# Filling the edges of the second batch's value tile from GpSimd, ahead of the loads into the tile

## Chip, cores, metric

One core of one Trainium2 chip. The metric is the device time of one execution in microseconds, the median of several.

## The reference

Attention with a window of 32 and eight global tokens over 8 batches, 8 heads, 576 tokens of 64, then a gated feed-forward layer over all 4608 tokens:

```python
scores = scale * q @ k.T ; masked outside |i-j| <= 32 unless row or column is global
attn = softmax(scores) @ v                    # 8 x 8 x 576 x 64
x = attn.transpose(0, 2, 1, 3).reshape(4608, 512)
ffn_out = (gelu(x @ w_gate) * (x @ w_val)) @ w_out      # 512 -> 1536 -> 512
out = x + sigmoid(x @ w_res) * ffn_out
```

## The kernel before

The kernel runs in nine chunks of 512 tokens. For chunk c, TensorE does the feed-forward input products (`ffn_in`, twelve column blocks), then its output products (`ffn_out`), between which the attention of chunk c+1 is woven. The kernel puts TensorE's results into tiles in PSUM, and uses such a tile again once another engine has read it. Batch b's values lie in tile `ve[b % 2]`, with a column of ones per head (for the softmax sum) and zeroed edges; `vo` is a copy of it shifted by 64 tokens. The parts that matter (cuts are marked `# ...`):

```python
def load_v(b):                       # five loads, f32 in HBM -> bf16, on GpSimd's queue
    t = ve[b % 2]
    for c in range(5):
        # ... rows p0:p1 of block c
        nc.gpsimd.dma_start(t[p0:p1, c, :, 0:D], v[b].rearrange("h s d -> s h d")[s0 + p0:s0 + p1])

def shift_v(b):                      # copy within the chip's memory, SyncE's queue
    nc.sync.dma_start(vo[b % 2][0:64, 0:4, :, :], ve[b % 2][64:128, 0:4, :, :])
    nc.sync.dma_start(vo[b % 2][64:128, 0:4, :, :], ve[b % 2][0:64, 1:5, :, :])

def zero_rest(i, eng):
    eng.memset(ve[i][:, :, :, D:VG], 1.0)
    eng.memset(ve[i][0:32, 0, :, :], 0.0)
    eng.memset(ve[i][96:128, 4, :, :], 0.0)
    eng.memset(gt[i][:, 0:64], 0.0)
    eng.memset(gt[i][:, 64 + S:128 + S], 0.0)
    eng.memset(ptg[i][:, :, 64 * (i % 2):64 * (i % 2) + 64], 0.0)
# ...
load_qk(1)                           # all on GpSimd's queue, in this order
load_gate_cols(1024, 1536)           # last third of wg_t and wv_t
load_v(1)
nc.gpsimd.dma_start(wr_t, moe_w_res.rearrange("(kt p) n -> p kt n", p=128))
for h0 in range(0, NFF, 6):          # wo_t in two halves
    nc.gpsimd.dma_start(wo_t[:, h0:h0 + 6, :], moe_w_out.rearrange("(kt p) n -> p kt n", p=128)[:, h0:h0 + 6, :])
for n in range(1, B // 2):
    for what in "kqv":
        gather(what, n)              # nine gathers
# ... attention of chunk 0
for c in range(NCH):
    # ... transposes of q and k of batch c+1 (SyncE); load_v(c+1) if c > 0
    for j in range(NFF):
        ffn_in(c, j)                 # g_ps, v_ps on TensorE; gelu on ScalarE; ht = gsb * v_ps on VectorE
        if c == 0 and j == 1:        # (shortened)
            zero_rest(1, nc.vector)
            hot_rows(1)
        # ... at j == 8: shift_v(c+1), load_qk(c+2), copies qz of q
    # 16 slots: scores, global rows (sn), values (nd) and transposes (xt) of chunk c+1,
    # each followed by one of: r_ps (gate), f_ps in three groups of four matmuls; four times
```

At the end of `ffn_out` VectorE makes `prb`, GpSimd adds `ob = prb + xtok`, and SyncE's queue stores `ob`. The transposes `xt` of the next chunk stand on that same queue between the stores.

The softmax here doesn't subtract the row's maximum and nothing guards it: scores larger than these inputs give would overflow.

Of the kernel before, what the change touches and what calls it, by code (L numbers as in the profile page):

```python
# [23 lines left out]
def kernel(  # L24
# [12 lines left out]
    nc = tc.nc  # L37
# [48 lines left out]
    def load_qk(b):  # L86
        for src, dst in ((q, q_st), (k, k_st)):
            for r in range(NQT):
                n = min(128, S - 128 * r)
                nc.gpsimd.dma_start(dst[0:n, r, :].rearrange("p (h d) -> p h d", d=D),  # L90
                                    src[b].rearrange("h s d -> s h d")[128 * r:128 * r + n])

    def load_v(b):
        t = ve[b % 2]
        for c in range(5):
            p0, p1 = (32, 128) if c == 0 else (0, 96) if c == 4 else (0, 128)
            s0 = 128 * c - 32
            nc.gpsimd.dma_start(t[p0:p1, c, :, 0:D],  # L98
                                v[b].rearrange("h s d -> s h d")[s0 + p0:s0 + p1])

    def shift_v(b):
        nc.sync.dma_start(vo[b % 2][0:64, 0:4, :, :], ve[b % 2][64:128, 0:4, :, :])
        nc.sync.dma_start(vo[b % 2][64:128, 0:4, :, :], ve[b % 2][0:64, 1:5, :, :])

    def load_gate_cols(n0, n1):
        for src, dst in ((moe_w_gate, wg_t), (moe_w_val, wv_t)):
            nc.gpsimd.dma_start(dst[:, :, n0:n1], src.rearrange("(kt p) n -> p kt n", p=128)[:, :, n0:n1])
# [46 lines left out]
    def zero_qk(i):  # L154
        for u in range(2):
            zero_wide(qz[i], 64 - 64 * u, 64, u * S, [[2 * S, NP], [1, S]])
        zero_wide(kt[i], 0, 128, 0, [[S + 64, NP], [1, 32]])
        zero_wide(kt[i], 0, 128, 32 + S, [[S + 64, NP], [1, 32]])
# [9 lines that stand above are left out]
    def zero_globals(b0, b1):  # L168
        zero_wide(kgz, 0, 128, b0 * NP * 128, [[1, (b1 - b0) * NP * 128]])
        zero_wide(qgz, 0, 128, b0 * NP * 16, [[1, (b1 - b0) * NP * 16]])  # L170
# [58 lines left out]
    def hot_rows(i):  # L229
        r0 = 64 - 64 * (i % 2)  # L230
        nc.scalar.copy(gt[i][r0:r0 + 64, 64:64 + S], hot[r0:r0 + 64, :])
# [6 lines left out]
    def double_qk(n0, n1):  # L238
        for what in "kq":
            nc.vector.tensor_copy(twice[what][:, n0:n1, :, :],  # L240
                                  view(gath[what], 0, 128, n0 * D, [[D, n1 - n0], [0, 2], [1, D]]))

    def spread_qk(n0, n1):
        nn = n1 - n0
        for what, big, pstep in (("k", kgz, 144), ("q", qgz, 16)):
            tg = pss.tile([128, nn, 128], BF16, name="tg", tag="sc")
            for n in range(nn):
                nc.tensor.transpose(tg[:, n, :], twice[what][:, n0 + n, :, :].rearrange("p a d -> p (a d)"), ident)
            width = big.shape[2] * big.shape[3]
            for e in range(2):  # L250
                shift = 64 * e if what == "k" else 0
                for u in range(2):
                    (nc.scalar.copy if what == "q" else nc.vector.tensor_copy)(
                        view(big, 64 * u, 64, (2 * n0 + e) * width + shift + 8 * u,
                             [[2 * width, nn], [pstep, NP], [1, NG]]),
                        view(tg, 64 * u, 64, 64 * e + 8 * u, [[128, nn], [16, NP], [1, NG]]))

    def spread_v(n0, n1):
        nc.vector.tensor_copy(vgb[:, n0:n1, 0:D], gath["v"][:, n0:n1, :])

    def spread_vg(b, eng):
        r0 = 64 * (b % 2)
        eng.tensor_tensor(vgs[r0:r0 + 64, b, :].rearrange("p (h e) -> p h e", e=VG),
                          view(vgb, r0, 64, (b // 2) * VG, [[0, H], [1, VG]]),
                          view(diag, r0, 64, 0, [[1, H], [0, VG]]), ALU.mult)
# [32 lines left out]
    def turn_qk(b):  # L298
        for src, dst, c0 in ((q_st, qt[b % 2], 0), (k_st, kt[b % 2], 32)):
            for r in range(NQT):  # L300
                n = min(128, S - 128 * r)
                nc.sync.dma_start(dst[:, :, c0 + 128 * r:c0 + 128 * r + n], src[0:n, r, :], transpose=True)

    def prep_qz(b, p0, p1):
        for u in range(2):
            nc.vector.tensor_copy(qz[b % 2][64 * u:64 * u + 64, p0:p1, u, :],  # L306
                                  qt[b % 2][64 * u:64 * u + 64, p0:p1, :])
# [93 lines left out]
    def ffn_in(c, j):  # L401
        x = xt[c % 2]
        g_ps = psm.tile([128, 512], F32, name="g_ps", tag="mm")
        for kk in range(NKT):
            nc.tensor.matmul(g_ps, wg_t[:, kk, 128 * j:128 * j + 128], x[:, kk, :],  # L405
                             start=(kk == 0), stop=(kk == NKT - 1))
        v_ps = psm.tile([128, 512], F32, name="v_ps", tag="mm")
        for kk in range(NKT):
            nc.tensor.matmul(v_ps, wv_t[:, kk, 128 * j:128 * j + 128], x[:, kk, :],  # L409
                             start=(kk == 0), stop=(kk == NKT - 1))  # L410
        gsb = work.tile([128, 512], BF16, name="gsb", tag="gsb", bufs=3)
        nc.scalar.activation(gsb, g_ps, ACTF.Gelu, bias=0.0, scale=1.0)  # L412
        nc.vector.scalar_tensor_tensor(ht[:, j, :], gsb, 0.5, v_ps, ALU.mult, ALU.mult)  # L413
# [58 lines left out]
    global_rows(0)  # L472
    load_qk(1)
    load_gate_cols(1024, 1536)
    load_v(1)
    nc.gpsimd.dma_start(wr_t, moe_w_res.rearrange("(kt p) n -> p kt n", p=128))
    for h0 in range(0, NFF, 6):
# [17 lines left out]
    for c in range(NCH):  # L495
        b = c + 1
        if b < B:
            if c == 0:
                zero_qk(1)
            turn_qk(b)  # L500
            if b > 1:
                load_v(b)
        held = None
        for j in range(NFF):
            ffn_in(c, j)
            if b < B:
                if c == 0:
                    if j == 1:
                        zero_rest(1, nc.vector)
                        hot_rows(1)  # L510
                    elif j == 2:
                        zero_globals(2, B)
                        spread_vg(1, nc.vector)
                if c == 1:
                    if j == 3:
                        double_qk(1, B // 2)
                    elif j == 6:
                        spread_qk(1, B // 2)
                        spread_v(1, B // 2)
                    elif j == 8:  # L520
                        for n in range(2, B):
                            spread_vg(n, nc.gpsimd)
                if j == 8:
                    shift_v(b)
                    if b + 1 < B:
                        load_qk(b + 1)
                    prep_qz(b, 0, NP)
                if j == 11:
                    held = global_scores(b)
        slots = {n: [] for n in range(16)}  # L530
        if c + 1 < NCH:
            if held is not None:
                slots[0].append(lambda: global_exp(b, *held))
                slots[4].append(lambda: global_rows(b))
            for n in range(8):
                slots[n].append(lambda n=n: scores(c + 1, n // 4, n % 4))
            for t in range(4):
                slots[5 + 2 * t].append(lambda t=t: values(c + 1, t))
                slots[7 + 2 * t].insert(0, lambda t=t: turn_x(c + 1, t))
        work_f = [w for t in range(4) for w in ffn_out(c, t)]  # L540
        for n in range(16):
            for w in slots[n]:
                w()
            work_f[n]()
# [30 lines left out]
```

## Time and profile before

| | before |
|---|---|
| time, median (range) | 433.5 us (432.9 to 435.0, 4 runs) |
| span in the profile | 431.6 us |
| TensorE busy | 386.6 us, 90% |
| VectorE, ScalarE, GpSimd busy | 49%, 39%, 39% |
| TensorE idle for ht, from 44 us on | 20.2 us |
| granted clock at one half | 20.5 us, from 47.6 to 68.1 |

In the profile, a wait reads "who <- for whom: us in total, times, longest"; a timeline row reads "start, duration, engine, line of the kernel, operation, written <- read, count", with the idle time ahead of it in brackets. PE is TensorE, DVE VectorE, ACT ScalarE, POOL GpSimd, SPq SyncE's DMA queue; `in_v` is v in HBM, the chip's main memory. The granted clock is the share of its full clock that TensorE was given. The lines for the stall are in the prediction. One more view is needed for the comparison, SyncE's queue in the kernel before:

```profile
62.00 0.47 SPq L102 DMA_DIRECT2D vo<-ve  x1
...
85.65 0.38 SPq L440 DMA_DIRECT2D out_dram<-ob  x1
88.03 1.21 SPq L393 DMA_TRANSPOSE xt<-xtok  x1
```

The first store goes out 2.4 us before the first transpose: here the store does not hold the transpose up.

### The profile page before, as it was taken

The page shows a single profiled execution, that of the slowest core. Times are in us where ns is not written, and L with a number is a line of the kernel's source. Part 1 is how long each engine was busy: PE and PEld are TensorE (multiplying, and loading weights), DVE is VectorE, ACT ScalarE, POOL GpSimd, SP SyncE. Part 2 cuts the span into 40 slices and gives each one's busy share as a digit, 9 for nine tenths or more (in the row PEclk, how much of TensorE's full clock was granted, in tenths as well). Part 3 has the DMA queues.
Part 4 walks back from the last instruction along what each step waited for, and adds up shares of the span by engine and source line. Part 5 has one row for each costly group of instructions (what it writes and reads, how often), then busy time and mean ns, then how long its engine had stood idle before and what let it go on. Part 6 is the DMA issues. An engine that isn't in the chain of part 4 may idle for free.

```text
span 431.6 us, 7189 instructions
## 1 busy us (share of the span) xinstructions
PE 386.6 (90%) x2749; PEld 208.9 (48%) x2794; DVE 209.6 (49%) x396; ACT 169.6 (39%) x274; POOL 167.9 (39%) x194
## 2 busy tenths in 40 slices
PE   2578009999999999999999999999999999999995
PEld 1363004654465446544654565456545654564442
DVE  6774027554656355535544554356435644463421
ACT  5455002623462336333623462345235423533320
POOL 6577252915492471257125712561330120022012
PEclk9999758999999999999999999999999999999999
DMA  7999998949997999399849992996296130021001
GB/s 173 169 178 155 161 164 170 109 93 112 146 92 111 101 178 120 66 124 182 88 87 112 185 89 77 128 184 73 74 147 93 38 98 1 0 75 62 0 26 74
DMA packets 164642, 46.56 MB, mean 108 GB/s; under 512 B 152128, under 2 KB 158784, under 8 KB 164608
## 3 DMA queue, kind: packets, MB, share of 16 engines
q0 software_dynamic: 108784, 18.62, 60.5%
q1 hardware_dynamic: 55824, 27.48, 33.0%
q8 instruction: 22, 0.36, 0.4%
q14 instruction: 12, 0.10, 0.1%
HBM read 39.19 MB, written 9.44 MB: 113 GB/s over the span
## 4 chain that ended last, share of the span: by engine, by line
PE 74%; issue 8%; POOL 1%; DVE 1%; POOLq 0%; DVEq 0%
PE f_ps L432 19%; PE v_ps L409 18%; PE g_ps L405 17%; PE r_ps L422 6%; PE nd L373 4%; PE sc L347 3%; PE nd L367 2%; PE sn L335 2%; PE sg L313 2%; POOL ob L438 1%; PE ss L318 1%; DVE qz L306 1%; PE tx L397 0%; POOLq L570 0%; DVE ht L413 0%
## 5 line engine op out<-in xcount | busy, mean ns | idle before, releaser
L409 PE MATMUL v_ps<-xt,wv_t 128*128 128x512 bf16 x431 | 111.8, 382 | 21.0 <-DVE ht L413 20.4
L412 ACT ACTIVATE gsb<-g_ps 128x512 bf16<-128x512 f32 x108 | 64.5, 597 | 145.8 <-PE g_ps L405 112.4
L413 DVE SCALAR_TENSOR_TENSOR ht<-gsb,v_ps 128x512 bf16<-128x512 bf16 x108 | 73.9, 687 | 91.7 <-PE v_ps L409 90.1
L438 POOL TENSOR_TENSOR ob<-prb,xtok 128x512 f32<-128x512 f32 x36 | 41.9, 1164 | 193.3 <-DVE prb L436 193.2
L405 PE MATMUL g_ps<-xt,wg_t 128*128 128x512 bf16 x415 | 109.4, 381 | 1.1 <-ACT xt L398 0.7
L432 PE MATMUL f_ps<-wo_t,ht 128*128 128x512 bf16 x412 | 102.0, 380 | 1.0
L409 PEld LDWEIGHTS <-wv_t 128*128 128x128 bf16 x432 | 42.5, 98 | 72.5 <-issue 22.3
L405 PEld LDWEIGHTS <-wg_t 128*128 128x128 bf16 x432 | 42.4, 98 | 52.0 <-issue 1.9
L432 PEld LDWEIGHTS <-ht 128*128 128x128 bf16 x432 | 38.4, 98 | 34.0
L350 ACT ACTIVATE pt<-sc 128x512 bf16<-128x512 f32 x72 | 41.8, 597 | 29.1 <-PE sc L347 29.0
L425 ACT ACTIVATE rsb<-r_ps 128x512 bf16<-128x512 f32 x36 | 21.4, 596 | 62.0 <-PE r_ps L422 58.0
L352 DVE TENSOR_TENSOR pt<-pt,maskw 128x512 bf16<-128x512 bf16 x72 | 31.8, 444 | 26.7 <-ACT pt L350 25.6
L90 POOL DMA_DIRECT2D q_st<-in_q_dram x35 | 29.8, 868 | 24.0 <-DMA qt<-q_st 24.0
L436 DVE SCALAR_TENSOR_TENSOR prb<-rsb,f_ps 128x512 f32<-128x512 bf16 x36 | 24.6, 684 | 29.4 <-PE f_ps L432 29.2
L422 PE MATMUL r_ps<-wr_t,xt 128*128 128x512 bf16 x137 | 36.6, 379 | 0.4
L98 POOL DMA_DIRECT2D ve<-in_v_dram x40 | 34.3, 869 | 1.9 <-DMA k_st<-in_k_dram 1.9
L90 POOL DMA_DIRECT2D k_st<-in_k_dram x35 | 30.8, 908 | 2.8 <-issue 1.2
L347 PE MATMUL sc<-qz,kt 128*128 128x128 bf16 x288 | 27.8, 224 | 0.0
L347 PEld LDWEIGHTS <-kt 128*128 128x128 bf16 x288 | 21.7, 100 | 12.1
L387 DVE TENSOR_TENSOR xtok<-nd,rden 128x512 bf16<-128x512 f32 x34 | 23.5, 692 | 1.2
L373 PEld LDWEIGHTS <-pt 128*128 128x128 bf16 x576 | 22.3, 97 | 1.8 <-DMA vo<-ve 0.8
L373 PE MATMUL nd<-ve,pt 128*128 128x65 bf16 x320 | 22.4, 193 | 0.0
(104 smaller groups left out, 259.7 us busy)
## 6 DMA issues: line engine op xcount, KB each, us to landing
out_dram<-ob SPq DMA_DIRECT2D x36, 256.0 KB, 2.1
vo<-ve SPq DMA_DIRECT2D x16, 260.0 KB, 5.7
q_st<-in_q_dram POOLq DMA_DIRECT2D x28, 128.0 KB, 5.0
k_st<-in_k_dram POOLq DMA_DIRECT2D x28, 128.0 KB, 6.1
ve<-in_v_dram POOLq DMA_DIRECT2D x24, 128.0 KB, 6.7
ve<-in_v_dram POOLq DMA_DIRECT2D x16, 96.0 KB, 6.0
wg_t<-in_moe_w_gate_dram POOLq DMA_DIRECT2D x3, 512.0 KB, 5.9
wv_t<-in_moe_w_val_dram POOLq DMA_DIRECT2D x3, 512.0 KB, 12.7
```

The source lines that it names most:

```text
L90: nc.gpsimd.dma_start(dst[0:n, r, :].rearrange("p (h d) -> p h d", d=D), src[b].rearrange("h s d -> s h d")[128 * r:128 * r + n])
L98: nc.gpsimd.dma_start(t[p0:p1, c, :, 0:D], v[b].rearrange("h s d -> s h d")[s0 + p0:s0 + p1])
L347: nc.tensor.matmul(sc[:, n, :, :], kt[b % 2][:, p, 64 * i:64 * i + 128], qz[b % 2][:, p, :, 64 * i:64 * i + 64], start=True, stop=True)
L350: nc.scalar.activation(mine, sc, ACTF.Exp, bias=0.0, scale=SCALE)
L373: nc.tensor.matmul(nds[h // 4][:, VG * (h % 4):VG * (h % 4) + VG], view(pt, 0, 128, c0, [[1, 128]]), vw, start=False, stop=(h % 4 == 3 and ...
L405: nc.tensor.matmul(g_ps, wg_t[:, kk, 128 * j:128 * j + 128], x[:, kk, :], start=(kk == 0), stop=(kk == NKT - 1))
L409: nc.tensor.matmul(v_ps, wv_t[:, kk, 128 * j:128 * j + 128], x[:, kk, :], start=(kk == 0), stop=(kk == NKT - 1))
L412: nc.scalar.activation(gsb, g_ps, ACTF.Gelu, bias=0.0, scale=1.0)
L413: nc.vector.scalar_tensor_tensor(ht[:, j, :], gsb, 0.5, v_ps, ALU.mult, ALU.mult)
L422: nc.tensor.matmul(r_ps, xt[c % 2][:, kk, 128 * t:128 * t + 128], wr_t[:, kk, :], start=(kk == 0), stop=(kk == NKT - 1))
L432: nc.tensor.matmul(held["f"], ht[:, j, 128 * t:128 * t + 128], wo_t[:, j, :], start=(j == 0), stop=(j == NFF - 1))
L438: nc.gpsimd.tensor_tensor(ob, prb, xtok[c % 2][:, t, :], ALU.add)
```

## The change

The six memsets of batch 1 stood on VectorE, behind the value loads in program order. The change puts them ahead of the loads, on the engine that issues the loads.

```diff
     load_gate_cols(1024, 1536)
+    zero_rest(1, nc.gpsimd)
     load_v(1)
@@
                     if j == 1:
-                        zero_rest(1, nc.vector)
                         hot_rows(1)
```

## The prediction

> **What bounds the kernel now.** I read the page first. Its second part shows TensorE (PE) at nine tenths or more in every slice from the seventh on, and its fifth part, the groups, has PE at the top with costs that the change does not touch. The only large hole is in slices five and six (each is 431.6 / 40 = 10.8 us), where PE falls to 0 and its granted clock to 0.5:
>
> ```profile
> PE   2578009999999999999999999999999999999995
> ...
> PEclk9999758999999999999999999999999999999999
> ```
>
> The table of waits for the stretch from 30 to 100 us then names who held whom (total us, times, longest):
>
> ```profile
> DVE ve L161 <- DMA ve<-in_v_dram: 23.1, 1, 23.1
> ...
> ACT gsb L412 <- DVE ht L413: 21.4, 1, 21.4
> PE v_ps L409 <- DVE ht L413: 20.4, 2, 20.2
> ...
> POOL kgf L191 <- DMA wo_t<-in_moe_w_out_dram: 4.8, 1, 4.8
> ...
> POOL qgf L191 <- DMA wo_t<-in_moe_w_out_dram: 2.6, 1, 2.6
> ```
>
> One memset on VectorE (DVE) waits 23.1 us for the loads into the value tile of batch 1, because it writes the same tile after them in program order. DVE is in order, so the products ht behind it wait too, PSUM banks stay full, and PE stops. The timeline gives the times (start, duration, engine, line, work, idle before):
>
> ```profile
> 38.06 0.69 DVE L413 SCALAR_TENSOR_TENSOR ht<-gsb,v_ps 128x512 bf16<-128x512 bf16 x1 [1.05 <-PE v_ps L409]
> 61.88 0.09 DVE L161 MEMSET ve<- 128x40 bf16 x1 [23.14 <-DMA ve<-in_v_dram]
> ...
> 63.53 0.63 DVE L413 SCALAR_TENSOR_TENSOR ht<-gsb,v_ps 128x512 bf16<-128x512 bf16 x1
> ```
> ```profile
> 42.97 1.03 PE L405 MATMUL g_ps<-xt,wg_t 128*128 128x512 bf16 x4
> 64.21 1.87 PE L409 MATMUL v_ps<-xt,wv_t 128*128 128x512 bf16 x4 [20.22 <-DVE ht L413]
> ...
> 80.13 1.03 PE L432 MATMUL f_ps<-wo_t,ht 128*128 128x512 bf16 x4
> ...
> 81.22 1.03 PE L432 MATMUL f_ps<-wo_t,ht 128*128 128x512 bf16 x4
> ...
> 98.82 1.03 PE L405 MATMUL g_ps<-xt,wg_t 128*128 128x512 bf16 x3
> ```
>
> So the stall is 20.2 us. But it does not follow that 20 us come back. During the stall GpSimd's DMA queue went on loading weights, and the second group of lines in the waits says so: two gathers wait for wo_t. The same timeline for GpSimd:
>
> ```profile
> 49.68 0.82 POOL L478 DMA_DIRECT2D wo_t<-in_moe_w_out_dram x1 [2.43 <-DMA wg_t<-in_moe_w_gate_dram]
> 52.62 0.82 POOL L478 DMA_DIRECT2D wo_t<-in_moe_w_out_dram x1 [2.11 <-DMA wv_t<-in_moe_w_val_dram]
> ...
> 69.58 0.94 POOL L191 DMA_INDIRECT kgf<-in_k_dram,idx  x1 [4.79 <-DMA wo_t<-in_moe_w_out_dram]
> 73.16 1.52 POOL L191 DMA_INDIRECT qgf<-in_q_dram,idx  x1 [2.64 <-DMA wo_t<-in_moe_w_out_dram]
> ...
> 84.34 1.29 POOL L438 TENSOR_TENSOR ob<-prb,xtok 128x512 f32<-128x512 f32 x1
> ```
>
> The program's list of waits lets each load on this queue start only when the load eight before it has landed. So these rows date landings: the last third of wg_t by 49.7, of wv_t by 52.6, the first half of wo_t at 69.6, the second at 73.1. wr_t's eighth follower, at 63.84, waits for nothing, so wr_t is there by 63.8. In the table of stretches the queue moves 200 to 255 GB/s until 73 us and 12 GB/s from 73 to 76: the backlog ends with wo_t.
>
> **What the Trainium skill says.** (1) "DMA: Bandwidth & Descriptors", anatomy of one DMA, GpSimd path: DMA engines do not wait on semaphores, the issuing sequencer does, and the engines consume their queues. The trace agrees: wo_t, issued at 52.62, lands 20.3 us later, behind what was queued before it. (2) "GPSIMD Engine Reference", key points: VectorE is structurally about twice as fast for elementwise work. The trace agrees in part: the ones take 290 ns on GpSimd and 92 on DVE, but a 32x520 zero takes 521 and 492. (3) "TensorE: Matmul & The Clock Gate", part 1: an idle window of some 3.4 us halves the clock, and a busy one restores it. The trace agrees: PE stops at 44.0, the clock falls at 47.6 (0.81 in the microsecond from 47 to 48); work resumes at 64.2, the clock is full at 68.1.
>
> **The change part by part.** *Removed from DVE:* six memsets, 92 + 492 + 492 + 85 + 85 + 192 ns = 1.4 us, and the wait of 23.1 us. *Added to GpSimd:* the same six, which the trace has for batch 0 at 7.96 to 9.99 us: 2.0 us. They now stand before the five value loads, in GpSimd's order, with no DMA to wait for. Before, these loads were issued at 38.33 (three in a row), 41.96 and 43.61, the last two after waits on older loads. Now the first three go out at about 40.4 to 42.9, the fourth about 43.0, the fifth about 43.9, and wr_t still at 46.5, after a wait on the queue. The value loads cannot move before wv_t lands (52.6), so a 2 us later issue costs nothing; wo_t lands as before. Cost on the path: about 0.
>
> *What PE then does.* Groups of four matmuls take 0.863 us, a pair g, v 1.73 us. From 43.9 it goes on to the end of column block 7 at 34.2 + 8 x 1.73 = 48.0. Block 8 needs the last thirds: wg_t by 49.7, wv_t by 52.6; then v of block 8 and three more pairs, 0.86 + 3 x 1.73 = 6.1, end near 58.7. The global scores need the transposed k, whose last issue ends at 53.64 with a median landing of 5.1, so about 58.7 as well; scores end near 60.5. The gate matmul waits for wr_t, about 63 to 64. Then f_ps waits for wo_t: four matmuls at 69.6, one scores group, two more f_ps, and the third of the next group needs the second half (its block is number 6): 73.1. Before, that matmul ran two steps of 0.216 after 81.22, at 81.65. **The ceiling of the gain is 81.65 - 73.1 = 8.5 us,** not 20.
>
> *What is lost again.* PE idles some 5.5 us before 69.6, which probably halves its clock; it restarts at 69.6, and by the 3.9 us that the restart took before it is full at 73.5, later if the short gap at 72.5 counts against it. Half-speed work after 73.1 costs 0.2 to 1 us: I take 0.5.
>
> Then the next feed-forward stage (98.82 before) needs three transposes of the attention output, issued on SyncE's queue in order with the output stores: store 0, transpose 0, store 1, transposes 1 and 2. Store 0 waits for ob, and GpSimd gets to ob only at 84.34 because it is issuing ten loads from 75.9 to 84.3, tied to wo_t and not to PE. Before, prb was ready then anyway (83.48 + 0.68). Now it waits. ob 0 ends 85.6, ob 1 86.8, store 1 about 87, transposes 1 and 2 from 87.3 to 90.1 (2.84 us for the two before), the last lands some 2.6 after its issue begins at 88.7: 91.3. With a gain of 8.0 the stage would start at 90.8, so this takes 0.5, perhaps 1.5 if the loads still in flight slow it. I take 0.7.
>
> Sum: 8.5 - 0.5 - 0.7 = 7.3 us. From 100 to 400 us PE is over 99% busy and everything there moves along. 433.8 - 7.3 = **426.5 us**, 1.7% less.
>
> **The rivals.** *A, the whole stall comes back:* 20.2 plus the cold restart (13 groups took 13.1 us instead of 11.2, so 1.9) less nothing: about 412. For it: the waits table names only this wait. Against it: f_ps cannot run before its weights land, at 73.1 by GpSimd's own waits; it would need wo_t to arrive 13 us earlier, and nothing in the change takes bytes from the queue. *B, the wait moves and more is lost:* PE's hour of need collides with loads, the transposes arrive late (DMA queues under load took 5 to 10 us for a transpose of k), and the gain is 3 to 4: about 430. For it: SyncE's and GpSimd's orders are both fixed, and the stage after is fed through both. Against it: the loads of batch 2 have drained by 88.4 in the trace, just as the transposes would start. *C, the memsets hold up the queue by their 2.0 us after all,* and wo_t lands at 75: gain about 5.5, time about 428. Against it: the backlog of 15 us (37.59 to 52.6 for wv_t) is in front of them. *D, within noise of nothing:* only if the trace's landings of wo_t were delayed equally by PE's work; nothing in it shows that.
>
> **Range and chances.** The ceiling of 8.5 makes 425.3, just short of 2% (8.7 us, 425.1). To pass it wo_t must land a little earlier or my clock and transpose losses be zero with noise on top: 0.15. B's and C's ends give the high edge, 430; the low edge, 424.3, allows wo_t to land 1 us earlier with no loss. Slower by over 2% would need a new stall of over 16 us: 0.02.
>
> **What would show it.** Right: no DVE wait for in_v; the six memsets on GpSimd near 38.3 to 40.4 us; wo_t waits of the gathers still ending near 69.6 and 73.2; a new wait of PE (or of its weight loads) on DMA wo_t of 5 to 6 us, and a short one; PE clock low around 68 to 74 instead of 48 to 68; the second feed-forward stage starting at 91 to 92 instead of 98.8. Wrong: f_ps running well before 69 us (then A, and my reading of the landings fails); wo_t landing past 75 (C); the second stage starting later than 93.5 with PE waiting on transposes (B).

## The result, and the profile after

| | before | after |
|---|---|---|
| time, median | 433.5 us | 427.06 us (426.92 to 427.44, 4 runs) |
| span | 431.6 | 425.2 |
| v of column block 5 (counted from 0) on TensorE | 64.21 | 43.77 |
| first f_ps | 80.13 | 70.25 |
| f_ps that needs wo_t's second half | 81.65 (81.22 + 2 x 0.216) | 73.57 |
| second feed-forward stage begins | 98.82 | 92.39 |

The ratio is 0.9847 (95% interval 0.9820 to 0.9874): by the interval a gain of 1.3 to 1.8%. Ratios here and below are the mean time of one kernel's runs over that of the other's of the same rounds, so not quite the ratio of the medians quoted. Executions over 1.5% slower than the fastest of the same kernel are left out of the means.

The page's part 2 of the kernel after, to set against the two lines of before (a slice is now 10.6 us):

```profile
PE   2578675999999999999999999999999999999994
...
PEclk9999995999999999999999999999999999999998
```

The hole of almost two empty slices has become a shallow one, and the clock's dip has moved later and halved. The waits between 30 and 100 us show what stands in the place of VectorE's wait for `in_v`, which is gone:

```profile
PE f_ps L432 <- DMA wo_t<-in_moe_w_out_dram: 5.2, 2, 5.0
...
PE v_ps L409 <- DMA wv_t<-in_moe_w_val_dram: 2.1, 1, 2.1
...
PE r_ps L422 <- DMA wr_t<-in_moe_w_res_dram: 1.9, 1, 1.9
...
PE g_ps L405 <- DMA wg_t<-in_moe_w_gate_dram: 1.3, 1, 1.3
...
PE g_ps L405 <- DMA xt<-xtok: 0.8, 1, 0.8
```

TensorE now catches up with the loads and waits for each weight tensor in the order of GpSimd's queue. The timeline of GpSimd after, for the rows that the prediction showed of before:

```profile
49.75 0.82 POOL L479 DMA_DIRECT2D wo_t<-in_moe_w_out_dram  x1 [1.98 <-DMA wg_t<-in_moe_w_gate_dram]
52.84 0.82 POOL L479 DMA_DIRECT2D wo_t<-in_moe_w_out_dram  x1 [2.27 <-DMA wv_t<-in_moe_w_val_dram]
...
70.46 0.94 POOL L191 DMA_INDIRECT kgf<-in_k_dram,idx  x1 [5.13 <-DMA wo_t<-in_moe_w_out_dram]
73.79 0.94 POOL L191 DMA_INDIRECT qgf<-in_q_dram,idx  x1 [2.39 <-DMA wo_t<-in_moe_w_out_dram]
...
84.42 2.41 POOL L438 TENSOR_TENSOR ob<-prb,xtok 128x512 f32<-128x512 f32 x2
```

Each row lies within 0.9 us of before. The DMA queue hardly noticed the change; only TensorE did. TensorE's rows after:

```profile
70.25 1.89 PE L432 MATMUL f_ps<-wo_t,ht 128*128 128x512 bf16 x4 [5.00 <-DMA wo_t<-in_moe_w_out_dram]
...
73.57 1.01 PE L432 MATMUL f_ps<-wo_t,ht 128*128 128x512 bf16 x2 [0.16 <-DMA wo_t<-in_moe_w_out_dram]
...
88.87 2.75 PE L432 MATMUL f_ps<-wo_t,ht 128*128 128x512 bf16 x12
92.39 1.02 PE L405 MATMUL g_ps<-xt,wg_t 128*128 128x512 bf16 x4 [0.77 <-DMA xt<-xtok]
```

The first row took 1.89 us where a warm group of four has 1.03: half clock. The last row is the second wait, and SyncE's queue after shows where it comes from:

```profile
61.47 0.46 SPq L102 DMA_DIRECT2D vo<-ve  x1
...
85.74 0.38 SPq L440 DMA_DIRECT2D out_dram<-ob  x1
86.23 1.22 SPq L393 DMA_TRANSPOSE xt<-xtok  x1
```

The first store still goes out at 85.7, because GpSimd gets to `ob` only at 84.42; but the attention output that the transpose needs was there at 80.5 (it was made from 79.83 in 0.69 us). Now the store holds the transpose up.

### The profile page after: what moved, and what is told of

It is laid out like the page before. It is cut to its first block, busy times and chain, and to the rows that moved or that the text cites. A ratio compares the mean times of both kernels' runs of the same rounds, so it can differ in the third digit from the quotient of the medians.

```text
span 425.2 us, 7233 instructions
## 1 busy us (share of the span) xinstructions
PE 390.8 (92%) x2794; PEld 209.4 (49%) x2794; DVE 208.7 (49%) x390; ACT 169.8 (40%) x274; POOL 170.3 (40%) x200
## 4 chain that ended last, share of the span: by engine, by line
PE 72%; DMA 14%; issue 8%; DVE 2%; POOL 2%; SPq 1%; ACT 0%; POOLq 0%; DVEq 0%
PE f_ps L432 19%; PE g_ps L405 16%; PE v_ps L409 16%; PE r_ps L422 6%; DMA wv_t<-in_moe_w_val_dram 5%; DMA wo_t<-in_moe_w_out_dram 5%; PE nd L373 4%; PE sc L347 3%; DMA wo_t<-in_k_dram 2%; PE nd L367 2%; PE sg L313 2%; PE sn L335 2%; POOL ob L438 1%; DVE qz L306 1%; PE ss L318 1%
## 5 line engine op out<-in xcount | busy, mean ns | idle before, releaser
L405 PE MATMUL g_ps<-xt,wg_t 128*128 128x512 bf16 x432 | 110.9, 379 | 2.7 <-DMA wg_t<-in_moe_w_gate_dram 1.3
L432 PE MATMUL f_ps<-wo_t,ht 128*128 128x512 bf16 x432 | 107.7, 384 | 5.2 <-DMA wo_t<-in_moe_w_out_dram 5.2
```

Of the source, the lines that this page charges most:

```text
L405: nc.tensor.matmul(g_ps, wg_t[:, kk, 128 * j:128 * j + 128], x[:, kk, :], start=(kk == 0), stop=(kk == NKT - 1))
L432: nc.tensor.matmul(held["f"], ht[:, j, 128 * t:128 * t + 128], wo_t[:, j, :], start=(j == 0), stop=(j == NFF - 1))
```

## The experiments

Twelve kernels ran, all with correct results. "Before" in their ratios was run beside them.

**1. The memsets ahead of the loads, but on VectorE.**

```diff
-    zero_rest(1, nc.gpsimd)
+    zero_rest(1, nc.vector)
     load_v(1)
```

> The change with its other half undone: the six memsets stand ahead of the loads into the value tile, but on VectorE instead of GpSimd. Theory (what counts is the order against the loads, not the engine): no VectorE wait for in_v, the same new waits for wg_t, wv_t, wr_t and wo_t, first f_ps near 70.2 us, 427 us; up to 1.4 us more (428.5) if the memsets fall into a stretch of the attention stage in which TensorE waits for VectorE. Rival (GpSimd as the place is what helps, VectorE is freed of 1.4 us and of a wait): about 430 or above.

Measured: 427.84 us, ratio 0.9841 (0.9811 to 0.9871). First f_ps at 70.12, the one on the second half at 74.28. As the theory had it: the engine of the memsets does not matter here. It does not settle whether GpSimd's memsets make wo_t land slightly later than before: GpSimd has none here and wo_t landed no earlier, but the memsets now stand in VectorE's attention work (26.87 to 28.6) and the whole feed-forward stage starts 0.9 us later than in the change (35.17 against 34.28).

**2. The memsets on GpSimd, but behind the loads.** Against the kernel before:

```diff
                     if j == 1:
-                        zero_rest(1, nc.vector)
+                        zero_rest(1, nc.gpsimd)
```

> The other half alone: the six memsets go to GpSimd but stay behind the loads in program order. Rival (moving the work off VectorE is what helps): about 427, as in the change. Theory: VectorE's wait is gone and TensorE runs on as in the change up to f_ps at 70, but GpSimd reaches the memsets only after its gathers, near 76 to 78 us, and the copy of ve to vo waits for them (from 61.5 to about 78, landing near 84); the values of batch 1 then wait for vo until 84 instead of starting near 78.5. About 6 us of the gain of 6.4 are lost: 432 to 435.

Measured: 427.24 us, ratio 0.9822 (0.9784 to 0.9860; by the 2% rule unclear). My theory failed here: this half alone brings the whole gain too. TensorE's rows say why:

```profile
67.36 1.89 PE L432 MATMUL f_ps<-wo_t,ht 128*128 128x512 bf16 x4 [2.52 <-DMA wo_t<-in_moe_w_out_dram]
...
71.28 0.59 PE L432 MATMUL f_ps<-wo_t,ht 128*128 128x512 bf16 x2 [0.87 <-DMA wo_t<-in_moe_w_out_dram]
...
75.78 1.29 PE L335 MATMUL sn<-ve,ptg 128*128 128x260 bf16 x10 [2.82 <-POOL ptg L166]
```

The memsets came late as expected (73.7 to 75.7) and the copy `vo` started at 74.0 instead of 61.5. But wo_t had landed by then: the copy's two halves landed in 3.1 and 3.7 us, against 5.8 and 6.6 in the changed kernel, where it runs beside the loads of wo_t. And wo_t, free of the copy, came 2.9 and 2.3 us earlier. What it won there it lost to the late memsets (2.82 us) and to the half clock that followed their gap (77.0 to 80.4). So two orders give the same time through different waits, and what both have in common, no wait of VectorE for `in_v`, is what the gain needs. Neither the engine nor the place alone is the cause.

**3 and 4. One more load ahead of wo_t, in the kernel after and in the one before.**

```diff
     nc.gpsimd.dma_start(wr_t, moe_w_res.rearrange("(kt p) n -> p kt n", p=128))
+    nc.gpsimd.dma_start(xt[1], moe_w_res.rearrange("(kt p) n -> p kt n", p=128))
```

> The changed kernel with one more load of 512 KB (a second copy of the residual weights into a tile not yet in use) put into GpSimd's queue between wr_t and wo_t. Theory (the landing of wo_t bounds this stretch): one such load took about 2.3 us (the last value load landed at 61.5, wr_t at 63.8), so f_ps starts 2.3 us later, and so does everything behind it: 427.1 + 2.3 = 429.4. Rival (TensorE's restart or something else bounds it, the load is hidden): within 0.5 us of 427.1.

> The same extra load in the kernel before. Theory: wo_t had 7 to 8 us of slack there (landed at 73.1, first needed at 80.1 and 81.6), so 2.3 us more are hidden: 433.5, within 0.5 us. Rival (the queue's total work sets the time in both): 435.8.

Measured: 429.95 us (ratio 0.9899, 0.9874 to 0.9924) in the kernel after, 434.12 (1.000, 0.9974 to 1.0025) in the one before. TensorE's rows in the kernel after with the extra load:

```profile
72.90 1.89 PE L432 MATMUL f_ps<-wo_t,ht 128*128 128x512 bf16 x4 [6.79 <-DMA wo_t<-in_moe_w_out_dram]
...
76.67 1.01 PE L432 MATMUL f_ps<-wo_t,ht 128*128 128x512 bf16 x2 [0.60 <-DMA wo_t<-in_moe_w_out_dram]
```

f_ps moved by 2.65 and 3.1 us and the time by 2.9 (2.3 by the ratios). Before, the same bytes cost nothing, though they moved wo_t there too: the gathers that wait for it start at 71.79 and 75.60 instead of 69.58 and 73.16, still ahead of f_ps. GpSimd's rows and the first f_ps of TensorE there:

```profile
71.79 0.94 POOL L191 DMA_INDIRECT kgf<-in_k_dram,idx  x1 [4.38 <-DMA wo_t<-in_moe_w_out_dram]
75.60 0.94 POOL L191 DMA_INDIRECT qgf<-in_q_dram,idx  x1 [2.87 <-DMA wo_t<-in_moe_w_out_dram]
```
```profile
79.65 1.03 PE L432 MATMUL f_ps<-wo_t,ht 128*128 128x512 bf16 x4
```

This is the cleanest evidence that the landing of wo_t bounds the stage after the change and did not before it. It does not tell by which path: the gathers wait for wo_t too, and the loads and `ob` behind them on GpSimd moved along (the first `ob` from 84.42 to 87.49). Run 6 separates the two.

**5. All four `ob` of the first chunk on VectorE,** to take the store out of the transposes' way.

```diff
-nc.gpsimd.tensor_tensor(ob, prb, xtok[c % 2][:, t, :], ALU.add)
+(nc.gpsimd if c else nc.vector).tensor_tensor(ob, prb, xtok[c % 2][:, t, :], ALU.add)
```

> The changed kernel with the last addition (ob) of the first chunk, four of 36, on VectorE instead of GpSimd. Theory (the store and the transposes on SyncE's queue wait for ob, which waits while GpSimd issues the loads of batch 2 until 84.4 us): ob is done near 77, store 0 near 77.5, transposes 1 and 2 right after the attention output is there, and the wait of 0.77 us (0.93 with the idle around it) ahead of the second feed-forward stage goes: 426.2, against 427.1. Cost on VectorE about 4 x 0.7 to 1.2 us, beside other work. Rival (the transposes are late because loads share the engines): no gain, 427.1.

Measured: 430.55 us, ratio 0.9944 (0.9922 to 0.9966): 3.5 us worse than the change (4.2 by the ratios), where the theory had 426.2 and the rival 427.1. Store 0 did go out at 76.9 and transposes 1 and 2 at 84.5. But GpSimd, rid of `ob`, ran straight on:

```profile
84.42 4.39 POOL L98 DMA_DIRECT2D ve<-in_v_dram  x5
```

In the changed kernel these five loads start at 93.62, held back only by the last `ob`. Started at 84.42 they share the DMA engines with the transposes, which took 8 us to land instead of 3.6. TensorE's row of the second stage in this run:

```profile
94.25 1.86 PE L405 MATMUL g_ps<-xt,wg_t 128*128 128x512 bf16 x4 [3.31 <-DMA xt<-xtok]
```

It waits 3.3 us and then runs at half clock. The rival, that loads slow the transposes, was the nearer one.

**6. Only the first two `ob` on VectorE,** so that the last two still hold those loads back.

```diff
-nc.gpsimd.tensor_tensor(ob, prb, xtok[c % 2][:, t, :], ALU.add)
+(nc.vector if c == 0 and t < 2 else nc.gpsimd).tensor_tensor(ob, prb, xtok[c % 2][:, t, :], ALU.add)
```

> The changed kernel with only the first two ob additions of the first chunk on VectorE; the last two stay on GpSimd, so its loads of the values of batch 2 cannot start before about 92. In the run with all four on VectorE they started at 84.4 and the transposes took 8 us to land instead of 3.6. Theory (with the loads held back, the transposes follow the attention output at once): the wait of 0.77 us for xt goes, the second feed-forward stage starts near 91.5 instead of 92.4: 426.2. Rival (VectorE's additions themselves cost the time, or the loads of q and k alone slow the transposes as much): 427 or more.

Measured: 426.14 us, ratio 0.9835 (0.9808 to 0.9862). The loads start at 94.06, the transposes are issued at 85.67 and land in 5.4 us, and the second stage begins at 91.93, right behind the last f_ps group:

```profile
89.34 2.75 PE L432 MATMUL f_ps<-wo_t,ht 128*128 128x512 bf16 x12
91.93 1.03 PE L405 MATMUL g_ps<-xt,wg_t 128*128 128x512 bf16 x4
```

The wait of 0.77 us is thus the store's, as the prediction had it; with it gone the stage follows f_ps at once. The time's gain over the change (0.9835 against 0.9847) is within the intervals, so this kernel is not shown to be faster.

**7. TensorE kept at work while it waits for wo_t:** 15 matmuls with unread results ahead of the first f_ps.

```diff
+if n == 0 and c == 0 and t == 0:
+    warm = psm.tile([128, 512], F32, name="warm", tag="mm")
+    for i in range(15):
+        nc.tensor.matmul(warm, wr_t[:, 0, 0:128], xt[0][:, 0, :], start=(i == 0), stop=(i == 14))
 if n == 0:
     held["f"] = psm.tile([128, 512], F32, name="f_ps", tag="mm")
```

> The changed kernel with 15 matmuls of 512 columns, whose result nobody reads, in the gap of TensorE between the gate matmul (65.0) and the first f_ps (70.25). Theory (the half clock from 64.7 to 74.9 us costs 0.7 us after wo_t has landed): the clock is full again by 68.1 or 71.5, f_ps starts at 70.2 as before, and 0.7 us come back: 426.4. If the fill runs past 70.2 some of it is lost. Rival (the clock costs nothing there because the loads bound it): 427.1.

Measured: 426.89 us, ratio 0.9848 (0.9824 to 0.9873): no gain. TensorE's rows:

```profile
69.38 1.02 PE L436 MATMUL f_ps<-wo_t,ht 128*128 128x512 bf16 x4 [1.15 <-DMA wo_t<-in_moe_w_out_dram]
...
73.33 1.01 PE L436 MATMUL f_ps<-wo_t,ht 128*128 128x512 bf16 x2 [2.28 <-DMA wo_t<-in_moe_w_out_dram]
74.14 0.63 PE L347 MATMUL sc<-qz,kt 128*128 128x128 bf16 x4
74.56 1.91 PE L436 MATMUL f_ps<-wo_t,ht 128*128 128x512 bf16 x4
```

The first group ran at full clock, but it was early for the second half of wo_t by 2.28 us, and in that gap the clock fell after all (half from 73.16 to 76.58). The idle time had only moved. The run does not take the clock's cost away, so it says nothing against it.

**8 and 9. All attention work of chunk 1 ahead of f_ps in the first chunk,** alone and with `ob` on VectorE:

```diff
+        if c == 0:
+            work_f[0]()                    # the first gate matmul
+            for n in range(16):            # scores, sn, nd, xt of chunk 1
+                for w in slots[n]:
+                    w()
+            for n in range(1, 16):
+                work_f[n]()
+            continue
```

> The changed kernel with another order of TensorE's work in the first chunk only: after the first gate matmul all the attention work of the next chunk (eight score groups, global rows, four value groups, four transposes) comes ahead of the f_ps matmuls. None of it needs wo_t. Theory (TensorE idles from 65 to 70.2 for wo_t): some 4 to 6 us of this work move into the gap, limited by the copy vo landing near 68 and by ScalarE's exponentials (8 x 0.6 us); the second feed-forward stage starts at 86.5 to 89 instead of 92.4: 421.5 to 424. Rival (the whole stretch is bound by the loads that follow, of batch 2): 426 to 427.

> attn_first with the first chunk's four ob additions on VectorE as well. With attn_first the products f_ps come closer together, and prb and ob have two buffers each, while GpSimd is busy issuing loads until 84.4 us; theory: 1 to 2 us better than attn_first, 420.5 to 423. Rival: same as attn_first, within 0.5 us.

Measured: 429.15 us (0.9898, 0.9875 to 0.9921) and 428.58 (0.9908, 0.9883 to 0.9934), both worse than the change. Without f_ps between them the value groups became a chain through VectorE: nd at 73.02, 75.81, 77.72 and 79.63, the last three waiting 0.6, 1.0 and 1.0 us for `xtok` (rows of run 8, whose profile is of the slowest of its six runs), and f_ps began only at 81.94, when wo_t had been there for 8 us. The expectation had counted TensorE's work, not the latency between its pieces. With `ob` on VectorE nothing is gained beyond the intervals, as that run's rival had it.

**10, 11, 12. The copy `vo` out of wo_t's way.** `shift_v(1)` is issued on GpSimd's queue behind wo_t (10), with the first two `ob` on VectorE as well (11), or with the ten loads of q and k of batch 2 moved behind the second `ob` and the last two `ob` on VectorE (12).

```diff
         nc.gpsimd.dma_start(wo_t[:, h0:h0 + 6, :], ...)      # both halves
+    shift_v(1, nc.gpsimd)                 # 10, 11, 12; no longer at j == 8 of the first chunk
@@ ffn_out
+    (nc.vector if c == 0 and t < 2 else nc.gpsimd).tensor_tensor(ob, ...)      # 11 only
+    (nc.vector if c == 0 and t >= 2 else nc.gpsimd).tensor_tensor(ob, ...)     # 12 only
@@ the 16 slots
             work_f[n]()
+            if c == 0 and n == 7:
+                load_qk(2)                # 12 only; no longer at j == 8 of the first chunk
```

> The changed kernel with the copy of batch 1's values (vo from ve, 520 KB) taken from SyncE's queue, where it starts at 61.5 us beside the loads of wo_t, and put on GpSimd's queue behind wo_t. In the run with the memsets behind the loads the copy started at 74.0 and the first half of wo_t landed near 67.4 instead of 70.2, the second near 71.3 instead of 73.5. Theory (the copy's bytes delay wo_t, and what then bounds the second feed-forward stage is GpSimd's loads of batch 2 ahead of ob): f_ps at 67.4, its third group's second half at 71.3, but the two more issues on GpSimd put ob 0 at about 85.4 and the transposes at 88.3 to 91, so the stage starts at 92 to 93.5 as now: 426.5 to 428. Rival (wo_t alone sets the time): 2.2 us better, 424.9.

> The two edits together: vo behind wo_t, and the first two ob additions on VectorE. Theory (each takes away the wait that hides the other's gain): wo_t's second half at 71.3, transposes of the attention output issued near 82 to 85 while the loads of q and k are still in flight until about 90, so they land near 90; second feed-forward stage at 89.5 to 91: 424.5 to 426, against 427.1. Rival (the queue's sum of bytes sets the time of the stage whatever the order): 427.

> The changed kernel with vo behind wo_t on GpSimd's queue, and the ten loads of q and k of batch 2 issued after the second ob addition of the first chunk instead of before the first (the last two ob additions of that chunk on VectorE, so that GpSimd is free to issue). Theory (wo_t first, then the transposes of the attention output, are the two waits in series; the loads of q and k are what makes the second late): wo_t near 67.4 and 71.3, ob 0 near 75, no loads in flight while the transposes run near 82 to 85, second feed-forward stage at 88.5 to 90 instead of 92.4; 2 us of that may be given back later, where VectorE's copies of q for batch 2 wait for transposes that now follow later loads: 423.5 to 426. Rival (what is gained in one place is given back in the next, as in the run with both edits): 427 to 428.

| run | time | ratio | wr_t there to f_ps, first / second half | f_ps on second half to last f_ps group | wait at the second stage |
|---|---|---|---|---|---|
| the change | 427.06 | 0.9847 | 6.5 / 9.8 us | 15.3 us | xt 0.77 |
| 10, vo behind wo_t | 428.17 | 0.9881 (0.9847 to 0.9916) | 3.8 / 8.8 | 16.1 | xt 2.28 |
| 11, with `ob` | 427.82 | 0.9874 (0.9845 to 0.9903) | 3.8 / 8.0 | 14.6 | xt 2.77 |
| 12, with q and k later | 427.37 | 0.9847 (0.9820 to 0.9873) | 3.8 / 8.1 | 17.0 | VectorE 1.6 |

Column four is measured from the start of r_ps, in whose row the wait for wr_t shows (in run 12, where a record is missing, from 63.79). It repeats what run 2 showed (3.8 and 7.7 there): without the copy beside it wo_t comes earlier. By how much has some scatter: of the runs that have the copy there, the change is at the slow end for the first half (runs 1, 5, 6 and 7 have 5.6, 5.7, 6.6 and 5.7 us, and 9.6 to 9.8 for the second half where a row shows it). So the copy had cost the first half 1.8 to 2.8 us and the second about 1 to 2. None of this reaches the end. What comes earlier is given back: in 10 to the transposes, which landed within 3.8 us (4.1 in the change) but still stood behind store 0, out only at 84.31 because GpSimd gets to `ob` at 82.99; in 11 to transposes that go out at 83.01 and land slowly (up to 7.6 us); and in 12 to the half clock and to a wait of the second stage on VectorE, busy there with prb and ob: the stretch from 71.86 to the last f_ps group took 17.0 us against 15.3 in the change, with the clock low until 76.93 against 74.92. Run 10 also scatters (425.4 to 430.6 over six runs; its profile is of a quick one, with wr_t there 2.9 us earlier than in the change), so its column reads are of one execution. No version here is shown to beat the change.

## Why the prediction was right

The time was predicted at 426.5 and measured at 427.06. The gain is the fairer measure: 7.3 us predicted, 6.4 measured. The time came closer than that only because the prediction took its gain from 433.8, the median of before as it then stood, and that median is now 433.5. By its steps:

- **The stall goes, but only up to wo_t.** Shown. The ceiling was put at 8.5 us; the f_ps on the second half moved from 81.65 to 73.57, 8.1 us, since TensorE got that half 0.4 us later than the 73.16 of before. Runs 3 and 4 show that this landing now bounds the time, and that it did not before.
- **The memsets cost nothing on the queue.** Nearly so. They ran from 38.19 to 40.24 as said, but the fifth value load was issued at 44.65 (said: 43.9) and wr_t at 47.01 (said: unchanged at 46.5). The gather that waits for wo_t's second half started at 73.79, 0.6 us later than before. Whether the memsets did that stays open. In runs 1 and 5 to 8, with the same loads, it started at 73.55 to 74.50, and in run 9, where wr_t too was 1.8 us earlier, at 72.07: 0.6 us is less than executions differ by.
- **The clock: 0.5 us.** The size is about right, the dating was not: it was low from 64.68 to 74.92, not from 68 to 74. From the f_ps on the second half to the last group took 15.30 us (88.87 - 73.57), before 14.58 (96.23 - 81.65), so 0.7. That agrees with an estimate from the clock record: 1.35 us at half clock after 73.57, half of which is lost. Run 7 could not take it away, so no experiment shows it.
- **The transposes behind the store: 0.7 us.** The second stage began 0.93 us after the last f_ps group's end (92.39 - 88.87 - 2.59). Run 6 shows that it is the store that waits for `ob`.
- **Sum.** 8.1 - 0.7 - 0.9 = 6.5, against 6.43 between the starts of the second stage and 6.4 between the spans. The prediction's 7.3 was too high by 0.9: 0.4 in the landing, 0.2 each in the clock and in the transposes, the rest rounding. All three err to the same side; nothing cancelled.
- **Misread, without effect here.** The queue moved 207 to 255 GB/s only from 61 to 70 us; from 49 to 61 it was 117 to 143, and from 70 to 73 it was 183. And the transposes of k were given their median over the whole run, 5.1 us from the last issue's end; the last one was there only at 61.3, not at 58.7, hidden behind wr_t at 63.78.
- **Rivals.** A (all 20 us come back) and C (wo_t at 75) did not happen. B had the right place but not the size.

What the prediction missed is not in its sum: the copy `vo` on SyncE's queue slows wo_t. It was in the trace of before, at 62.0 us beside the loads, and I treated the landing of wo_t as fixed by GpSimd's queue alone. Run 2 was mispredicted for that reason.

## What to carry to other kernels

A wait that is 20 us long is worth only the distance to the next wait behind it, and that one can be dated in the profile of the kernel before: from an in-order queue's own waits one can read when each transfer landed, and compare with when it was first needed. An operation off the critical path may be what holds back a transfer that would do harm; take it away only after looking at what its engine does next. Where several waits stand in series and share the DMA engines, moving one load only moved the wait here (runs 10 to 12); doubling a load ahead of the suspected one is a cheap test of whether it is binding, though all that waits for the load moves with it.

## What the Trainium skill lacked or had wrong

- "TensorE: Matmul & The Clock Gate", part 1, has the clock fall after an idle window of about 3.4 us, and the quick rule near the page's end is to have no idle gaps over some 3 us. In the changed kernel it fell at 64.68 though TensorE was busy for 1.40 of the 3.41 us before, and the longest idle stretch in them was 1.9 us (r_ps waiting for wr_t). The page mentions a kernel whose clock falls through frequent short idle stretches, but does not say how much work keeps the clock up. The window's length agrees: the stretches of half and full clock last 10.24, 20.48 and 40.96 us here, all multiples of 3.413.
- The same page's terms estimate the penalty as throttled time times (1 - K/N), which gives 5.1 us for the 10.24 us here. The stretch behind it became 0.7 us longer: TensorE waited for wo_t for 5.2 us of that time, and what ran slowly ahead of 73.57 was hidden behind that wait.
- "GPSIMD Engine Reference", key points, calls VectorE about twice as fast for elementwise work, and no page has the time of a memset on GpSimd. Here the two of 32x520 bf16 took 521 and 526 ns on GpSimd and 492 on VectorE. The others took 290, 156, 160 and 373 ns against 92, 85, 85 and 192, but of the last three VectorE writes half as many elements, of uint32 instead of bf16.
- "DMA: Bandwidth & Descriptors" describes the round robin between queues, but no page has what sharing costs a waiting consumer: a copy of 520 KB on SyncE's queue put the first half of wo_t 1.8 to 2.8 us later, and transposes beside the loads of v landed in 8 us instead of 3.6.
